# The first product of a layer by Strassen's seven products, with its elementwise function on four times wider tiles

## The chip, the cores and the metric

The kernel runs on one core of a Trainium2 chip. The metric is the device time of one execution in microseconds. TensorE (PE) does the matmuls, VectorE (DVE) and ScalarE (ACT) the elementwise work, GpSimd (POOL) a few reductions over partitions, and SyncE (SP) issues the transfers.

## The reference

Chunked attention makes 4608 rows of 512; two feed-forward layers follow, each 512 to 2048 to 512. The second layer is what the change is about:

```python
def _moe2_ref(x, w_in, w_out, a, b) -> np.ndarray:
    h = x @ w_in
    h2 = h * h
    h3 = h2 * h
    P = a[0] + a[1] * h + a[2] * h2 + a[3] * h3
    Q = 1.0 + np.abs(b[0]) * np.abs(h) + np.abs(b[1]) * h2
    g = P / (Q + 1e-06)
    return (g @ w_out).astype(np.float32)
```

The first layer has the same two products with `s * relu(h)**2 + b` between them. Everything is fp32 in and out; the weights come as 64-bit words and are decoded on the chip.

## The kernel before

Every product runs in pairs of fp16: an operand is scaled by a power of two and split in a high and a low half, and each product of 128x128 weights with a moving operand is made three times (`TERMS`: high by high, high by low, low by high) and added in PSUM.

Layer 1 goes through the rows in blocks (the list `blocks`: two of 256 rows in plain fp32, eight of 512). For each block it takes the 16 slices `f` of the 2048 inner columns: `l1_h` (L409 by `h_mm`: 12 matmuls of 512 columns into one PSUM bank), `l1_g` (Relu, Square and the split, whose low half is a subtraction on VectorE, L435), `l1_y` (L451: 12 matmuls into the four banks `y`). A table of jobs by slot (`at`) places attention, the decoding of weights (`w2_load`, `w2_park`) and, per block, `y_norm` and `y_split` (L374, L375) beside them. `y_split` splits the layer's result in four pieces and stores it to DRAM (`yd`). In the last block the weights of layer 2 are fetched again and split, two a slot (`split`, L172 and L173).

Layer 2 takes nine blocks of 512 rows. A unit is one slice `f` of a block: `l2_s1` makes h (12 matmuls, `h_mm`, banks h, h, s, x in turn) and starts the rational function on 128x512 elements, `l2_s2` ends it with the two halves of g, `l2_y` (L775) does 12 matmuls of the second product. The second product trails the first by `LAG = 3` units. The division is a logarithm and an exponential on ScalarE (L754, L755), followed by one correction for the low half. Per unit VectorE has seven operations (L750 to L752, L762 to L765) and ScalarE five.

The order on each engine is set by the framework's scheduler, which moves instructions within their dependences; the calls in the code set only their priority.

Of the kernel before, what the change touches and what calls it, by code (L numbers as in the profile page):

```python
# [20 lines left out]
def attn_moe_moe2(ctx: ExitStack, tc: tile.TileContext, qk, v, w_in, w_out, s_in, b_in,  # L21
# [39 lines left out]
    yd = [dram.tile([128, KD, 2, 512], F16, name=f"yd{j}", tag=f"yd{j}") for j in range(NB2)]  # L61
# [7 lines left out]
    def tiny(n, nm, dt=F32):  # L69
        return l1_p.tile([128, n], dt, name=nm, tag=nm)  # L70
# [119 lines left out]
    wo2 = Weight(w2_out, "out", None, "w")  # L190
# [90 lines left out]
    xhl = {}  # L281
# [203 lines left out]
    def y_norm(j2):  # L485
# [23 lines left out]

    def w2_scale():  # L510
# [48 lines left out]
    bufs = ((y1_p, "y32"), (y1_p, "yhl"), (raw_p, "raw"), (hl_p, "xhl"), (hl_p, "xhl"))[:3]  # L559
# [31 lines left out]
    at(start[2] + WS + WP * KF, w2_scale)  # L591

    if True:
# [63 lines left out]
        for slot, (j, f) in enumerate(seq1):  # L657
            if (j, f) == (NB - 1, 0):
                right.close()
                w2_p = ctx.enter_context(tc.tile_pool(name="w2", bufs=2 * KF + 1, side="right", reuse_waits="tile"))  # L660
                for w in (wi2, wo2):
                    w.pool = w2_p
                    for i in range(KF):
                        w.fetch(i)
            run_jobs(slot)
            if j == NB - 1:
                for n in (2 * f, 2 * f + 1):
                    w, i = park[n]
                    w.split(i)
# [12 lines left out]
        l2_p = ctx.enter_context(tc.tile_pool(name="l2", bufs=2, reuse_waits="tile"))
        o_p = ctx.enter_context(tc.tile_pool(name="o", bufs=4, reuse_waits="tile"))

        q0c = 1.0 + 1e-6
        bt = small(2)
        V.tensor_scalar(out=bt.bitcast(I32), in0=b2_sb.bitcast(I32), scalar1=0x7FFFFFFF, scalar2=None,
                        op0=ALU.bitwise_and)
        aabs = small(4)
        V.tensor_scalar(out=aabs.bitcast(I32), in0=a2_sb.bitcast(I32), scalar1=0x7FFFFFFF, scalar2=None,  # L690
                        op0=ALU.bitwise_and)
        rb = small(2)
        V.tensor_scalar(out=rb, in0=bt, scalar1=2.0 ** -100, scalar2=None, op0=ALU.max)
        V.reciprocal(out=rb, in_=rb)
        lnb = small(1)
# [142 lines left out]
```

## Time and profile before

| | |
|---|---|
| runs | 1621.27 us median of 3 (1620.11 to 1621.80) |
| profiled execution | 1621.44 us |
| its span, first to last instruction | 1619.7 us |
| mean granted TensorE clock, share of full | 0.995 |
| PE, DVE, ACT busy over the span | 99%, 76%, 60% |
| layer 1 and attention, to the last matmul of L451 | about 868 us |
| layer 2 | from there to the end |

A span is counted from the first to the last instruction. Times of one instruction are from its start to its end; neighbours on one engine can overlap, so the distance from start to start is the pace.

### The profile page before, as it was taken

The numbers are of one execution on the slowest core, as the hardware profiler recorded it, in microseconds if no ns is written. First come the engines' busy times: TensorE is split into PE (matmuls) and PEld (weight loads), VectorE is DVE, ScalarE is ACT, GpSimd is POOL, SyncE is SP. The second block draws the span as 40 slices with busy tenths as digits, with TensorE's granted clock in tenths as the row PEclk, the third lists the DMA queues.
The fourth block names the chain that finished last, engine by engine and source line by source line (L and its number), as shares of the span: only waits on it lengthen the run. The fifth ranks groups of instructions, "written<-read, shape, count | busy, mean of one in ns | idle before, by whom it ended". The sixth has DMA issues, their size and how long they took to land.

```text
span 1619.7 us, 25231 instructions
## 1 busy us (share of the span) xinstructions
PE 1604.5 (99%) x10052; PEld 795.6 (49%) x10052; DVE 1238.9 (76%) x2412; ACT 978.7 (60%) x1629; POOL 23.1 (1%) x57
## 2 busy tenths in 40 slices
PE   7999999999999999999999999999999999999999
PEld 6887454444444444444444444444444444444444
DVE  7986457766666664452456999999999999999997
ACT  3677556464645555453676666666666666666665
POOL 0000000000000000000000000000000000000000
PEclk8999999999999999999999999999999999999999
DMA  7732116435253522112501010101010101010000
GB/s 270 284 90 74 53 34 196 149 98 163 75 176 89 176 66 66 40 40 85 182 1 52 1 52 1 53 1 52 1 52 1 52 1 52 1 40 13 1 27 26
DMA packets 70549, 116.96 MB, mean 72 GB/s; under 512 B 37920, under 2 KB 37920, under 8 KB 68128
## 3 DMA queue, kind: packets, MB, share of 16 engines
q1 hardware_dynamic: 70432, 115.37, 22.0%
q8 instruction: 78, 1.28, 0.3%
q14 instruction: 39, 0.32, 0.1%
HBM read 79.70 MB, written 27.26 MB: 66 GB/s over the span
## 4 chain that ended last, share of the span: by engine, by line
PE 93%; DVE 3%; issue 3%; ACT 1%; POOL 0%; POOLq 0%
PE hp L409 43%; PE y L775 23%; PE y L451 20%; PE xp L296 2%; PE hp L419 1%; PE sp L248 1%; PE y L446 1%; DVE bits L134 1%; DVE wf L135 1%; DVE bits L132 1%; PE cs L479 0%; PE xp L354 0%; PE tp L311 0%; POOL amx L219 0%; DVE whl L173 0%
## 5 line engine op out<-in xcount | busy, mean ns | idle before, releaser
L409 PE MATMUL hp<-xhl,whl 128*128 128x512 f16 x3264 | 750.0, 380 | 0.0
L409 PEld LDWEIGHTS <-whl 128*128 128x128 f16 x3264 | 314.9, 98 | 375.9 <-issue 1.7
L775 PE MATMUL y<-whl,g 128*128 128x512 f16 x1728 | 395.4, 379 | 0.9 <-DVE g L762 0.5
L451 PE MATMUL y<-g,whl 128*128 128x512 f16 x1536 | 352.1, 379 | 0.0
L775 PEld LDWEIGHTS <-g 128*128 128x128 f16 x1728 | 168.6, 98 | 206.0 <-DVE g L765 3.0
L451 PEld LDWEIGHTS <-whl 128*128 128x128 f16 x1536 | 150.2, 98 | 181.6 <-issue 0.5
L754 ACT ACTIVATE rr<-qq,c 128x512 f32<-128x512 f32 x144 | 104.0, 722 | 194.9 <-DVE qq L750 194.7
L435 DVE TENSOR_TENSOR g<-r,g 128x512 f16<-128x512 f32 x128 | 88.0, 687 | 124.5 <-ACT g L434 124.5
L424 ACT ACTIVATE r<-hp 128x512 f32<-128x512 f32 (+1 forms) x160 | 87.5, 547 | 141.6 <-PE hp L409 126.2
L762 DVE SCALAR_TENSOR_TENSOR g<-e,na,rr 128x512 f16<-128x512 f32 x144 | 107.9, 750 | 17.1 <-ACT rr L755 14.6
L747 ACT ACTIVATE vv<-hp 128x512 f32<-128x512 f32 x144 | 85.5, 594 | 52.8 <-PE hp L409 52.6
L749 ACT ACTIVATE e<-hp,na 128x512 f32<-128x512 f32 x144 | 112.4, 780 | 0.0
L764 DVE SCALAR_TENSOR_TENSOR e<-e,na,qq 128x512 f32<-128x512 f32 x144 | 108.0, 750 | 3.8
L750 DVE SCALAR_TENSOR_TENSOR qq<-qq,bc,vv 128x512 f32<-128x512 f32 x144 | 107.2, 745 | 3.9 <-ACT qq L748 3.7
L752 DVE SCALAR_TENSOR_TENSOR e<-e,na,hp 128x512 f32<-128x512 f32 x144 | 107.3, 745 | 3.2
L755 ACT ACTIVATE rr<-rr,c 128x512 f32<-128x512 f32 x144 | 104.0, 722 | 4.5
L763 DVE SCALAR_TENSOR_TENSOR qq<-qq,g 128x512 f32<-128x512 f32 x144 | 99.5, 691 | 4.3
L765 DVE TENSOR_TENSOR g<-e,rr 128x512 f16<-128x512 f32 x144 | 99.2, 689 | 3.4
L748 ACT ACTIVATE qq<-hp,bc 128x512 f32<-128x512 f32 x144 | 98.1, 682 | 0.0
L751 DVE TENSOR_TENSOR e<-e,hp 128x512 f32<-128x512 f32 x144 | 97.8, 679 | 0.0
L425 ACT ACTIVATE r<-r 128x512 f32<-128x512 f32 (+1 forms) x160 | 93.5, 585 | 4.0
L434 ACT ACTIVATE g<-r 128x512 f16<-128x512 f32 x128 | 80.3, 628 | 3.2
(131 smaller groups left out, 1189.4 us busy)
## 6 DMA issues: line engine op xcount, KB each, us to landing
qk<-in_qk_dram SPq DMA_DIRECT2D x36, 512.0 KB, 4.0
raw<-in_moe_w_in_dram SPq DMA_DIRECT2D x16, 1024.0 KB, 5.3
raw<-in_moe_w_out_dram SPq DMA_DIRECT2D x16, 1024.0 KB, 5.2
v<-in_v_dram SPq DMA_DIRECT2D x36, 256.0 KB, 2.7
yd<-yhl SPq DMA_DIRECT2D x9, 1024.0 KB, 4.8
xhl<-yd SPq DMA_DIRECT2D x9, 1024.0 KB, 4.8
out_dram<-o SPq DMA_DIRECT2D x36, 256.0 KB, 2.1
w2din<-wf SPq DMA_DIRECT2D x16, 256.0 KB, 2.4
```

Source lines behind the costliest of these rows:

```text
L409: T.matmul(out=hp, lhsT=u[:, o:o + 128], rhs=x[:, kk, l, :], start=(m == 0), stop=(m == 3 * KD - 1))
L451: T.matmul(out=ybank[j][dd], lhsT=wo1.hl[f][:, o:o + 128], rhs=g[:, l, :], start=(f == 0 and m == 0), stop=(f == KF - 1 and m == 2))
L749: A.activation(out=e, in_=hp, func=AF.Identity, scale=na[:, 3:4], bias=na[:, 2:3])
L750: V.scalar_tensor_tensor(out=qq, in0=qq, scalar=bc[:, 0:1], in1=vv, op0=ALU.add, op1=ALU.mult)
L752: V.scalar_tensor_tensor(out=e, in0=e, scalar=na[:, 1:2], in1=hp, op0=ALU.add, op1=ALU.mult)
L754: A.activation(out=r, in_=qq, func=AF.Ln, scale=2.0 ** -40, bias=lnb)
L755: A.activation(out=r, in_=r, func=AF.Exp, scale=-1.0, bias=exb)
L762: V.scalar_tensor_tensor(out=g[:, 0, :], in0=e, scalar=na[:, 0:1], in1=r, op0=ALU.add, op1=ALU.mult)
L763: V.scalar_tensor_tensor(out=qq, in0=qq, scalar=q0c, in1=g[:, 0, :], op0=ALU.add, op1=ALU.mult)
L764: V.scalar_tensor_tensor(out=e, in0=e, scalar=na[:, 0:1], in1=qq, op0=ALU.add, op1=ALU.subtract)
L765: V.tensor_tensor(out=g[:, 1, :], in0=e, in1=r, op=ALU.mult)
L775: T.matmul(out=ybank[j][t], lhsT=g[:, a, t * 128:(t + 1) * 128], rhs=w[:, l * 512:(l + 1) * 512], start=(f == 0 and m == 0), stop=(f == KF ...
```

## The change

Layer 2's h is made in quadrants. The 512 inner dimensions are cut in two halves, the 512 rows of a block in two halves of 256 (`b`), the 2048 columns in two halves (`a`). Eight products of quadrants become seven, in Winograd's form of Strassen's method: sums of quadrants of the weights (`A11`, `A12`, `A22`, `S1` to `S4`) with sums of quadrants of the layer's input (`11`, `21`, `22`, `T1` to `T4`). The weights' sums are made and split once, in the last block of layer 1 (`w2_combo`, 28 tiles, in place of the 16 splits of `w2_in`); the input's sums in `y_split`, seven pieces (`y_piece`) in place of four.

A step is one quarter `u` of a block: seven products of 12 matmuls of 256 columns, into three PSUM banks Z, Y and C. Partial sums stay there: Z holds product 1, is copied to C (L968), then takes products 6, 5 and 3 on top, with ScalarE's and VectorE's copies between them: `snap` (L855), the add L982 (called H11), the add L984 (H10), and the copies L980 and L990. Together they fill `h`, 128x2048. The rational function then runs on all 2048 elements at once, as `chain_a` to `chain_e`; its denominator has a new form with one absolute value and one multiply-add. The second product (`l2_y`, now L907) is the same, and trails two steps; `m4` puts its four slices of a step into four slots between the products. The first and the last step's chains run in four parts of 512. `wo2` is fetched and split while layer 1's last block frees buffers. `hl` has ten buffers of quarter size.

```diff
+    PROD = {"1": ("A11", "11"), "2": ("A12", "21"), "3": ("S4", "22"), "4": ("A22", "T4"),
+            "5": ("S1", "T1"), "6": ("S2", "T2"), "7": ("S3", "T3")}
...
     def y_split(j2):
-        hl = y1_p.tile([128, KD, 2, 512], F16, name="yhl", tag="yhl")
-        split_hl(hl, y32.pop(j2), scy)
-        nc.sync.dma_start(out=yd[j2], in_=hl)
+        for p in YORD:
+            y_piece(j2, p)
...
+        if p == "T3":
+            src = y1_p.tile([128, 2, 256], F32, name="tx", tag="tx")
+            V.tensor_tensor(out=src, in0=b22, in1=b12, op=ALU.subtract)
...
+        hl = y1_p.tile([128, 2, 2, 256], F16, name="yhl", tag="yhl", bufs=3)
+        A.activation(out=hl[:, 0], in_=src, func=AF.Identity, scale=scy)
+        V.scalar_tensor_tensor(out=hl[:, 1], in0=src, scalar=scy, in1=hl[:, 0], op0=ALU.mult, op1=ALU.subtract)
+        nc.sync.dma_start(out=yd[j2][p], in_=hl)
...
+        def product(i, p, b, start, stop=False):
+            j, u = seq[i]
+            wk, pk = PROD[p]
+            for s in range(2):
+                f = 2 * u + s
+                for kk in range(2):
+                    w = wi2.sh[wk, kk, f // 4]
+                    for n, (a, l) in enumerate(TERMS):
+                        o = (f % 4) * 128
+                        T.matmul(out=b[:, s, :], lhsT=w[:, a, o:o + 128], rhs=yin[j][pk][:, l, kk, :],
...
+        def chain_b(i, sl):
...
+            V.scalar_tensor_tensor(out=v, in0=v, scalar=dlt, in1=v, op0=ALU.add, op1=ALU.mult)
+            V.tensor_tensor(out=e, in0=e, in1=hh, op=ALU.mult)
+            V.scalar_tensor_tensor(out=e, in0=e, scalar=na[:, 1:2], in1=hh, op0=ALU.add, op1=ALU.mult)
...
+        for i in range(N + 2):
+            cur, c = i < N, i - 1
+            sl = (parts if c in (0, N - 1) else full) if 0 <= c < N else []
...
+                product(i, "1", Z, True)
+                product(i, "7", Y, True)
...
+            for x in sl:
+                chain_a(c, x)
+            for x in sl:
+                chain_b(c, x)
+            run_m4(i, 0)
+            if cur:
+                C = new_bank(i, "C")
+                A.activation(out=C, in_=Z, func=AF.Copy)
+                product(i, "2", C, False)
+                product(i, "6", Z, False)
+            for x in sl:
+                chain_c(c, x)
+                chain_d(c, x)
...
+            run_m4(i, 1)
+            if cur:
+                snap(i, "u1", Z)
+                snap(i, "p7", Y)
+                A.activation(out=hq[:, 0, 0], in_=C, func=AF.Copy)
+                product(i, "5", Z, False)
+                V.tensor_tensor(out=hq[:, 1, 1], in0=Z, in1=sn.pop((i, "p7")), op=ALU.add)
+                product(i, "4", Y, False, True)
+                V.tensor_tensor(out=hq[:, 1, 0], in0=Y, in1=sn.pop((i, "u1")), op=ALU.add)
+            if len(sl) == 1:
+                chain_e(c, sl[0])
+            run_m4(i, 2)
+            if cur:
+                product(i, "3", Z, False, True)
+                A.activation(out=hq[:, 0, 1], in_=Z, func=AF.Copy)
+            run_m4(i, 3)
```

In the middle of layer 2 VectorE's row holds, before, one unit after another; this is the rest of one and the start of the next, with small operations of `l2_par` between them:

```order
L762 SCALAR_TENSOR_TENSOR g_12123<-e,na,rr 128x512
L763 SCALAR_TENSOR_TENSOR qq<-qq,g_12123 128x512
L764 SCALAR_TENSOR_TENSOR e<-e,na,qq 128x512
L765 TENSOR_TENSOR g_12123<-e,rr 128x512
L737 TENSOR_TENSOR ao<-ig,c_130 128x1
L727 TENSOR_SCALAR ig<-ge 128x1
L750 SCALAR_TENSOR_TENSOR qq<-qq,bc,vv 128x512
L751 TENSOR_TENSOR e<-e,hp 128x512
L752 SCALAR_TENSOR_TENSOR e<-e,na,hp 128x512
```

And this, at the same place on VectorE, is one whole step of the change (called v, eh, e2, g0, v2, e3, H11, H10 and g1 in the text):

```order
L873 SCALAR_TENSOR_TENSOR v<-v,c_262 128x2048
L874 TENSOR_TENSOR e<-e,h 128x2048
L875 SCALAR_TENSOR_TENSOR e<-e,na,h 128x2048
L888 SCALAR_TENSOR_TENSOR g_12176<-e,na,r 128x2048
L889 SCALAR_TENSOR_TENSOR v<-v,g_12176 128x2048
L895 SCALAR_TENSOR_TENSOR e<-e,na,v 128x2048
L982 TENSOR_TENSOR h<-bZ,sn 128x2x256
L984 TENSOR_TENSOR h<-bY,sn 128x2x256
L896 TENSOR_TENSOR g_12176<-e,r 128x2048
```

The seven operations stay seven, each four times as wide, and the two adds that fill h of the next step stand between the sixth and the seventh.

At the start of layer 2, the end of the first chain (in parts of 512) on VectorE, and what stands behind it:

```order
L888 SCALAR_TENSOR_TENSOR g_10423<-e,na,r 128x512
L895 SCALAR_TENSOR_TENSOR e<-e,na,v 128x512
L889 SCALAR_TENSOR_TENSOR v<-v,g_10423 128x512
L896 TENSOR_TENSOR g_10423<-e,r 128x512
L895 SCALAR_TENSOR_TENSOR e<-e,na,v 128x512
L982 TENSOR_TENSOR h<-bZ,sn 128x2x256
L896 TENSOR_TENSOR g_10423<-e,r 128x512
L984 TENSOR_TENSOR h<-bY,sn 128x2x256
```

The adds of step 1 stand at the very end of step 0's chain; before, no add stood on VectorE between a product and its use.

In layer 1 this is `y_split` of one block on VectorE before (`c_196` is its scale, g the subtraction L435):

```order
L375 SCALAR_TENSOR_TENSOR yhl<-y_5106,c_196,yhl 128x512 x2
L435 TENSOR_TENSOR g<-r,g 128x512
L375 SCALAR_TENSOR_TENSOR yhl<-y_5106,c_196,yhl 128x512 x2
L97 TENSOR_SCALAR apm<-amx 128x1
L99 TENSOR_SCALAR ape<-apm 128x1
```

And after (the same subtraction is now L440; two of the sums, T3 and T1, already stand ahead of these rows):

```order
L440 TENSOR_TENSOR g<-r,g 128x512
L524 SCALAR_TENSOR_TENSOR yhl<-y_5287,c_250,yhl 128x512 x2
L524 SCALAR_TENSOR_TENSOR yhl<-tx,c_250,yhl 128x512
L101 TENSOR_SCALAR apm<-amx 128x1
L516 TENSOR_TENSOR tx<-y_5287 128x512
L103 TENSOR_SCALAR ape<-apm 128x1
L519 TENSOR_TENSOR y_5287<-tx,y_5287 128x2x256
L524 SCALAR_TENSOR_TENSOR yhl<-y_5287,c_250,yhl 128x512 x2
L440 TENSOR_TENSOR g<-r,g 128x512
L524 SCALAR_TENSOR_TENSOR yhl<-tx,c_250,yhl 128x512
```

Seven wide splits and four sums now stand about the subtractions g where four splits stood.

## Rows read from the trace of the kernel before

**Rows 1.** The page, part 1: TensorE's busy time, share and instructions.

```profile
PE 1604.5 (99%) x10052; PEld 795.6 (49%) x10052; DVE 1238.9 (76%) x2412; ACT 978.7 (60%) x1629; POOL 23.1 (1%) x57
```

**Rows 2.** The page, part 4: the chain that ended last.

```profile
PE 93%; DVE 3%; issue 3%; ACT 1%; POOL 0%; POOLq 0%
PE hp L409 43%; PE y L775 23%; PE y L451 20%; PE xp L296 2%; PE hp L419 1%; PE sp L248 1%; PE y L446 1%; DVE bits L134 1%; DVE wf L135 1%; DVE bits L132 1%; PE cs L479 0%; PE xp L354 0%; PE tp L311 0%; POOL amx L219 0%; DVE whl L173 0%
```

**Rows 3.** Busy time by windows, 950 to 1600 us: stretch, length, each engine, clock.

```profile
950.00:1600.00 650.00, 650.00 (x3013) 294.71 (x3012) 614.40 (x977) 426.53 (x659) 0.00 (x0) 1.00 0.06 23
```

**Rows 4.** Timeline of VectorE in layer 2: start, duration, line, operation, count.

```profile
902.22 0.74 DVE L762 SCALAR_TENSOR_TENSOR g<-e,na,rr 128x512 f16<-128x512 f32 x1
902.88 0.74 DVE L750 SCALAR_TENSOR_TENSOR qq<-qq,bc,vv 128x512 f32<-128x512 f32 x1
903.54 0.68 DVE L763 SCALAR_TENSOR_TENSOR qq<-qq,g 128x512 f32<-128x512 f32 x1
904.15 0.68 DVE L751 TENSOR_TENSOR e<-e,hp 128x512 f32<-128x512 f32 x1
...
906.67 0.74 DVE L762 SCALAR_TENSOR_TENSOR g<-e,na,rr 128x512 f16<-128x512 f32 x1
```

**Rows 5.** The chain that ended last in order of time: start, length, matmuls.

```profile
228.23 3.20 PE cs L479 x128
...
1605.41 10.38 PE y L775 x48
```

**Rows 6.** Groups by line and form: busy us, mean ns of one, idle before.

```profile
L775 PE MATMUL y<-whl,g 128*128 128x512 f16 x1728 | 395.4, 379 | 0.9 <-DVE g L762 0.5 <-DVE g L765 0.4
...
L731 DVE TENSOR_TENSOR na<-na,c 128x1 f32<-128x1 f32 x27 | 4.2, 155 | 0.3
...
L479 PEld LDWEIGHTS <-whl 128*128 128x128 f16 x128 | 3.4, 96 | 0.2
```

**Rows 7.** Groups by line and form on VectorE and ScalarE, two sizes each.

```profile
L751 DVE TENSOR_TENSOR e<-e,hp 128x512 f32<-128x512 f32 x144 | 97.8, 679 | 0.0
L425 ACT ACTIVATE r<-r 128x512 f32<-128x512 f32 x128 | 80.4, 628 | 3.4
L260 DVE TENSOR_TENSOR e<-sp,mx 128x256 f32<-128x256 f32 x72 | 27.1, 413 | 0.0
L425 ACT ACTIVATE r<-r 128x256 f32<-128x256 f32 x32 | 13.2, 411 | 0.6
```

**Rows 8.** Timeline of VectorE at the end, where one operation needs the last.

```profile
1610.23 0.75 DVE L762 SCALAR_TENSOR_TENSOR g<-e,na,rr 128x512 f16<-128x512 f32 x1 [0.16 <-ACT rr L755]
1611.02 0.69 DVE L763 SCALAR_TENSOR_TENSOR qq<-qq,g 128x512 f32<-128x512 f32 x1
```

**Rows 9.** Timeline of ScalarE in layer 2.

```profile
900.93 0.60 ACT L747 ACTIVATE vv<-hp 128x512 f32<-128x512 f32 x1 [0.23 <-PE hp L409]
901.42 0.68 ACT L748 ACTIVATE qq<-hp,bc 128x512 f32<-128x512 f32 x1
901.99 0.78 ACT L749 ACTIVATE e<-hp,na 128x512 f32<-128x512 f32 x1
```

**Rows 10.** Timeline of TensorE where layer 2 begins.

```profile
868.03 10.52 PE L409 MATMUL hp<-xhl,whl 128*128 128x512 f16 x48
879.06 1.90 PE L775 MATMUL y<-whl,g 128*128 128x512 f16 x8 [0.51 <-DVE g L762]
```

**Rows 11.** Busy time by windows about L479: five engines, then the granted clock.

```profile
228.00:231.60 3.60, 3.60 (x131) 3.33 (x129) 2.01 (x9) 0.60 (x1) 0.38 (x1) 0.92 0.28 76
```

**Rows 12.** Busy time by windows, VectorE alone, layer 1 and its last block.

```profile
600.00:700.00 100.00, 48.36 (x115) 1.00 0.18 50
...
800.00:850.00 50.00, 28.74 (x40) 1.00 0.11 40
```

**Rows 13.** Timeline of VectorE and of TensorE at the end of layer 1.

```profile
857.23 0.69 DVE L435 TENSOR_TENSOR g<-r,g 128x512 f16<-128x512 f32 x1 [3.95 <-ACT g L434]
...
860.26 7.93 PE L451 MATMUL y<-g,whl 128*128 128x512 f16 x36
```

More of the change, by code (lines that the diff above doesn't have):

```diff
@@ L189, in attn_moe_moe2 @@
     wi2 = Weight(w2_in, "in", None, "w")
-    wo2 = Weight(w2_out, "out", None, "w")
+    wo2 = Weight(w2_out, "out", wo1_p, "w")
+    wi2.sh = {}
     park = [(w, i) for w in (wi2, wo2) for i in range(KF)]
@@ L408, in h_mm @@
                 o = a * 512 + (f % 4) * 128
-                T.matmul(out=hp, lhsT=u[:, o:o + 128], rhs=x[:, kk, l, :], start=(m == 0), stop=(m == 3 * KD - 1))
+                T.matmul(out=hp, lhsT=u[:, o:o + 128], rhs=x[kk][:, l, :], start=(m == 0), stop=(m == 3 * KD - 1))
                 m += 1
@@ L591, in attn_moe_moe2 @@
     at(start[2] + WS + WP * KF, w2_scale)
+    at(start[3], l2_consts)
     if True:
@@ L674, in attn_moe_moe2 @@
                 y_step()
+        for i in (KF - 2, KF - 1):
+            wo2.fetch(i)
         g_step()
@@ L677, in attn_moe_moe2 @@
             y_step()
-        for slot in sorted(jobs):
-            run_jobs(slot)
+        for i in range(KF - 4, KF):
+            wo2.split(i)
+        late = sorted(jobs)
         left.close()
[L682 to L695, printed above, removed]
-        V.memset(lnb, q0c * 2.0 ** -40)
-        exb = small(1)
-        V.memset(exb, -40.0 * 0.6931471805599453)
+        l2_p = ctx.enter_context(tc.tile_pool(name="l2", bufs=1, reuse_waits="tile"))
         yin = {}
@@ new lines, in chain_c, with chain_d @@
+        def chain_c(i, sl):
+            v, e, r = (t[:, sl[0]:sl[1]] for t in s2[i][:3])
+            A.activation(out=r, in_=v, func=AF.Ln, scale=2.0 ** -40, bias=lnb)
+            A.activation(out=r, in_=r, func=AF.Exp, scale=-1.0, bias=exb)
+        def chain_d(i, sl):
+            na, bc, ao = par[seq[i][0]]
+            if sl[0] == 0:
+                s2[i].append(l2_p.tile([128, 2, BIG], F16, name="g2", tag="g2", bufs=2))
+            v, e, r = (t[:, sl[0]:sl[1]] for t in s2[i][:3])
+            g = s2[i][3][:, :, sl[0]:sl[1]]
+            V.scalar_tensor_tensor(out=g[:, 0], in0=e, scalar=na[:, 0:1], in1=r, op0=ALU.add, op1=ALU.mult)
+            V.scalar_tensor_tensor(out=v, in0=v, scalar=q0c, in1=g[:, 0], op0=ALU.add, op1=ALU.mult)
@@ L770, in l2_y, with chain_e @@
+        def chain_e(i, sl):
+            na, bc, ao = par[seq[i][0]]
+            v, e, r = (t[:, sl[0]:sl[1]] for t in s2[i][:3])
+            g = s2[i][3][:, :, sl[0]:sl[1]]
+            V.scalar_tensor_tensor(out=e, in0=e, scalar=na[:, 0:1], in1=v, op0=ALU.add, op1=ALU.subtract)
+            V.tensor_tensor(out=g[:, 1], in0=e, in1=r, op=ALU.mult)
+        def l2_y(i, q):
+            j, u = seq[i]
+            if u == 0 and q == 0:
                 ybank[j] = [ps_y.tile([128, 512], F32, name=f"y{dd}", tag=f"y{dd}") for dd in range(4)]
-            g = s2.pop((j, f))
+            f = 2 * u + (q % 2) + 8 * (q // 2)
+            g = s2[i][3].rearrange("p l (q t) -> p l q t", q=4)
@@ new lines, in attn_moe_moe2 @@
+        T.matmul(out=prime, lhsT=wo2.hl[0][:, 0:128], rhs=wo2.hl[0][:, 0:512], start=True, stop=True)
+        N = len(seq)
+        full, parts = [(0, BIG)], [(a, a + 512) for a in range(0, BIG, 512)]
+        m4 = {i: [[], [], [], []] for i in range(N + 2)}
+        for i in range(N):
+            for q in range(4):
+                step, slot = i + 2, q
+                if i == 0:
+                    step, slot = ((2, 2), (2, 3), (2, 3), (3, 0))[q]
+                elif i == 1:
+                    slot = q
+                m4[step][slot].append((i, q))
```

238 lines of the change are left out of this document (167 added, 71 removed).

## The prediction

> **What bounds the kernel now.** I read the page's busy shares first, then the chain that ended last, then the second layer alone, and in it the pace of each engine.
>
> TensorE is busy 99% of the span and the chain that ended last is 93% TensorE [rows 1, 2]. Its three large lines are L409 (the first product of both layers), L775 (the second product of layer 2) and L451 (the second product of layer 1). In the window from 950 to 1600 us, which is nearly all of layer 2, TensorE is busy all 650 us, at full clock, VectorE 614 us and ScalarE 427 us [rows 3]. Busy time is no measure of room here, because consecutive operations overlap: the starts say more. On VectorE the seven operations of one unit of 128x512 start 4.45 us apart from one round to the next (902.22 to 906.67) [rows 4], while TensorE needs 24 matmuls, 2 x 2.59 = 5.18 us, for the same unit [rows 5]. So TensorE sets the pace of layer 2 and VectorE has 14% to spare; only fewer or shorter matmuls make it faster.
>
> Everything below is made against the profiled execution's own time, 1621.44 us (span 1619.7 and 1.7 around it), which lies 0.2 us above the median of the runs. What a measurement of this kernel can tell from no change is about 0.2%, 3.2 us.
>
> **The matmuls of layer 2.** Now: 144 units of 24 matmuls of 512 columns at 215.8 ns (48 in 10.38 us, so 12 in 2.59) [rows 5], so 745.8 us. The change keeps the second product (1728 matmuls of 512 columns, 373.0 us) and replaces the first one's 1728 by 36 steps x 7 products x 12 = 3024 matmuls of 256 columns. No row has a f16 matmul of 256 columns with a weight load of its own. Two rows bracket it. At best it costs half of one with 512, 107.9 ns. At worst I lay a straight line between the 128 matmuls of one column on L479, 3.20 us or 25.0 ns each, every one with its own 128x128 load, and the 512-column one: 25.0 + 190.8 x 255/511 = 120.2 ns. The L479 row says that loads follow each other at 25 ns although one takes 96 ns from start to end [rows 5, 6]: they are pipelined, and a load fits behind 107 ns of columns. So I take 109 ns, near the lower end: 329.6 us, **43.4 us less**. The bounds are 46.7 and 9.5 us less.
>
> Here a rule speaks against the change. The Trainium skill, "TensorE: Matmul & The Clock Gate", section "LDWEIGHTS (loading the stationary operand)", prices a load at its columns over 1.2 GHz, 107 ns for 128 columns, and its Part 3 says that a load overlaps a running matmul only where the two use different row groups. By that a matmul of 256 columns would be an estimated 107 + 107 = 214 ns, the price of 512 columns now, and the change would lose some 270 us. The trace disagrees: by the same rule 512 columns would cost 320 ns, and they are paced at 215.8; a pair on L479 takes 25.
>
> **One step of the changed layer 2.** A step is 7 x 1.31 + 4 x 2.59 = 19.5 us of TensorE, in place of 4 x 5.18 = 20.7. Do the others keep up?
>
> VectorE per step: seven operations of 2048 elements and two adds of 512. At 512 an operation with a per-partition scalar starts 0.66 us before the next, one without 0.60 [rows 4]. An element more costs (679 - 413)/256 = 1.04 ns [rows 7], so 1536 more cost 1.60 us: 2.26 and 2.20. Four of the first kind and three of the second make 15.6, the adds 1.2. Where an operation needs the one just before it, the start comes 0.79 instead of 0.66 after it [rows 8]: five such pairs, 0.6. The 24 small operations of `l2_par` come once in four steps and take at most 0.155 each [rows 6]: 0.9 a step. Sum 18.3 of 19.5: the large operations save four times 4.45 - 15.6 = 2.2 us of the fixed cost per step, and the adds take half of that back.
>
> ScalarE: 0.85 ns an element ((628 - 411)/256), 0.57 us from a 512-wide Abs with a pointer to the next start, 0.49 without [rows 7, 9]; so 1.9 to 2.0 us for each of four wide ones, five copies at 0.5, a quarter of four outputs: 11 us. It isn't near.
>
> The engines also wait for one another in a ring. `v` starts on VectorE; in the order shown, v, eh, e2, g0, v2, e3 and the add H11 (L982) follow, 2.26 + 2.20 + 2.38 + 2.39 + 2.33 + 2.38 + 0.60 = 14.5 us; product 3 may write its bank only then (1.3 and 0.2 drain); ScalarE empties it (0.5) and makes the next |h| (1.9), and the next `v` can start. That is 18.5 us with a semaphore's way or two, 1 us under the step. So TensorE stays the bound; for the outputs' four ScalarE operations between `v` and `e`, once in four steps, I add 2 us over the layer (bounds 0 and 9: 36 times a quarter of a microsecond).
>
> **Start of layer 2.** Today TensorE has 0.9 us of holes before the second product in all of layer 2 [rows 6], the first of 0.51 us at 879.06, after 48 matmuls of the first product [rows 10]. In the changed order the second product trails two steps, not three units. Let T be the end of layer 1's last product. The first step's h needs its seven products with the copies between them; its last add is done about T+10, ScalarE's first |h| half a microsecond later, and VectorE starts the first chain at T+11. That chain stands whole before the adds of step 1 (order shown), 4 x 4.45 + 1.2 = 19 us: T+30. Then follow 2.7 us of pieces of the last y and three rounds of 17.5 plus two y pieces. The low halves g1 of steps 1, 2 and 3 are ready at T+55, T+73 and T+91. Counted in the changed order, TensorE has before each of them 328, 395 and 467 short and 56, 104 and 152 long matmuls, 47.8, 65.5 and 83.7 us of work. It is 7 to 7.5 us early each time; from then on VectorE gains over 1 us a step and the hole doesn't grow. I take 8 us for it, **7 more than now**; bounds 3 (the early work stretches over it) and 15 (the clock falls too: it read 0.92 in 3.6 us with the one-column matmuls [rows 11]).
>
> **Layer 1.** `y_split` becomes seven pieces: 7 x 0.66 + 4 x 0.60 = 7.0 us of VectorE a block instead of 2.6, and seven ScalarE operations instead of four. What hides it: VectorE is busy 48 of 100 us there [rows 12], and in the order shown the pieces stand between the subtractions g that the second product needs. In the last block 28 weight combinations with 16 sums and 16 splits take the place of 32 splits, 38.6 against 21.1 us in 83; it is busy 29 of 50 [rows 12]. What cover a late g has: it ends at 857.92 and is read at 860.26, 2.3 us [rows 13]. Between two g's of the last block VectorE now has up to 7.7 us where a slot has 5.2, 2.5 late once. I take **2 us**; bounds 0 and 12. Without the cover it would be 8 x 4.4 = 35 us. SP's queue has seven transfers of 256 KB where one of 1 MB stood; ten `hl` buffers let the first three go at once, and each later one has a product before it.
>
> **End.** The last chain runs in four pieces beside the previous step's second product: its halves are ready 10.3 and 15.3 us after that begins, and TensorE asks at 10.4 and 15.6. **0.5 us**. ScalarE's four outputs and the last stores stay as they are.
>
> **Sum.** 1621.4 - 43.4 + 2 + 7 + 2 + 0.5 = 1589.5, so **1590 us**, 1.9% less.
>
> **The rivals.**
>
> *A load that is not hidden behind 256 columns.* For it: only 13 ns lie between 96 and 109, and nothing here has run so. Against it: 25 ns a pair on L479. At 120.2 ns the time is 1590 + 3024 x 0.0112 = 1624; with the load wholly exposed, 109 + 96 ns, it is 1880. By the skill's rule above the result would lie at that far end, which the 512-column pace contradicts.
>
> *The ring of three engines sets the step.* This one decides the sign. The spare in the ring is 1 us of 19.5; if the wide operations, or the waits between engines, add more than 1 us, TensorE waits in each of 36 steps. At 0.9 us over the spare, 1.9 in all, the gain of 31.5 us is gone; at 3 in all the time is 1590 + 72 = 1662. For it: VectorE's operations depend on each other, and a chain that was spread over three units in flight is now one. Against it: the prices above are read from rows, and the buffers of h, v and g are doubled.
>
> *Larger holes at the start and in layer 1*, from ScalarE's splits of `wo2` that wait for their fetches, or y pieces in the way: with 20 to 35 us more, 1610 to 1625. VectorE's 48% speaks against it.
>
> **How the numbers follow.** The forecast, TensorE bound with a hole at the start, 1578 to 1604: 66%. The load at 115 ns or more: 7%, two of them far out. The ring: 12%, half of it below the old time. Larger holes: 13%, three quarters faster. Below 1577: 2%. Together faster 0.83, same 0.06, slower 0.11. From 1577 to 1618 some 17% are left out.
>
> **What would show it.** Twelve matmuls of a product at 1.31 us in the timeline of TensorE; a step of 19.5 us with no wait in the steady part; VectorE's wide operations 2.2 to 2.3 us apart and its share near 90%; holes of 7 to 8 us in the first 60 us after layer 1 and none in it. I am wrong if product 3 or product 2 waits in every step (for the add L982 or the copy L968), if a product takes 1.4 us or more, or if layer 1 ends later than 868 us by more than a few.

## The result, and the profile after

The changed kernel takes 1594.66 us (median of four runs, 1593.01 to 1596.58) against 1621.53 us of the kernel before on the same chip: ratio 0.9835, 95% interval 0.9818 to 0.9852. The forecast was 1590 us, in a range of 1577 to 1618. The profiled execution took 1593.01 us, with a span of 1591.2 us. In what follows TensorE's pace is counted from start to start, 109.1 ns for a matmul of 256 columns and 215.8 ns for one of 512, and a hole is what lies between two groups beyond that pace.

The page, parts 1 and 4: busy time, and the chain that ended last.

```profile
PE 1565.9 (98%) x11349; PEld 923.6 (58%) x11349; DVE 1232.2 (77%) x1886; ACT 921.8 (58%) x1296; POOL 25.7 (2%) x57
...
PE 73%; DVE 16%; issue 4%; DMA 4%; ACT 3%; POOL 0%; SPq 0%; POOLq 0%; ACTq 0%; DVEq 0%
```

TensorE issues 1297 matmuls more than in [rows 1] and is busy 39 us less. It still ends the chain, but with 73% where [rows 2] had 93%: there are stretches in which VectorE decides. The next views tell where they are. TensorE in the steady part, start, duration, line and count:

```profile
1194.25 1.47 PE L849 MATMUL bZ<-xhl,whl 128*128 128x256 f16 x12
1195.56 1.47 PE L849 MATMUL bY<-xhl,whl 128*128 128x256 f16 x12
1196.87 2.75 PE L907 MATMUL y<-whl,g 128*128 128x512 f16 x12
...
1211.19 2.75 PE L907 MATMUL y<-whl,g 128*128 128x512 f16 x12
1213.78 1.47 PE L849 MATMUL bZ<-xhl,whl 128*128 128x256 f16 x12
```

A product takes 1.31 us (1195.56 to 1196.87), and product 1 comes again after 19.53 us, which is 7 x 1.31 + 4 x 2.59: TensorE waits for nothing and sets the pace. VectorE and ScalarE in the same step:

```profile
1182.07 2.35 DVE L888 SCALAR_TENSOR_TENSOR g<-e,na,r 128x2048 f16<-128x2048 f32 x1
1184.45 2.29 DVE L889 SCALAR_TENSOR_TENSOR v<-v,g 128x2048 f32<-128x2048 f32 x1
1186.78 2.35 DVE L895 SCALAR_TENSOR_TENSOR e<-e,na,v 128x2048 f32<-128x2048 f32 x1
1189.05 0.68 DVE L982 TENSOR_TENSOR h<-bZ,sn 128x512 f32<-128x512 f32 x1
1189.65 0.68 DVE L984 TENSOR_TENSOR h<-bY,sn 128x512 f32<-128x512 f32 x1
1190.25 2.28 DVE L896 TENSOR_TENSOR g<-e,r 128x2048 f16<-128x2048 f32 x1
...
1194.53 2.35 DVE L873 SCALAR_TENSOR_TENSOR v<-v,c 128x2048 f32<-128x2048 f32 x1 [1.14 <-ACT v L864]
```

```profile
1191.86 0.60 ACT L990 ACTIVATE h<-bZ 128x512 f32<-128x512 f32 x1 [8.03 <-PE bZ L849]
1192.49 2.00 ACT L864 ACTIVATE v<-h,bc 128x2048 f32<-128x2048 f32 x1
```

The wide operations start 2.20 to 2.38 us apart, as [rows 4, 7, 8] gave. The bracket on L873 is the ring of the prediction at work: the adds (1189.05 and 1189.65), product 3, the copy L990, the next `v`, and only then VectorE goes on. It stood idle 1.14 us for it.

TensorE where layer 2 begins, with the brackets of its waits, and its granted clock there (windows; the clock is the figure ahead of the last two):

```profile
883.65 1.47 PE L849 MATMUL bZ<-xhl,whl 128*128 128x256 f16 x12
888.04 2.29 PE L849 MATMUL bC<-xhl,whl 128*128 128x256 f16 x12 [2.91 <-ACT bC L968]
890.12 2.36 PE L849 MATMUL bZ<-xhl,whl 128*128 128x256 f16 x12
...
926.34 3.63 PE L907 MATMUL y<-whl,g 128*128 128x512 f16 x16 [0.75 <-DVE g L896]
...
945.30 3.63 PE L907 MATMUL y<-whl,g 128*128 128x512 f16 x16 [0.92 <-DVE m L807]
...
964.64 1.04 PE L907 MATMUL y<-whl,g 128*128 128x512 f16 x4 [0.96 <-DVE g L896]
```

```profile
884.00:888.00 4.00, 1.13 (x11) 0.86 (x9) 4.00 (x8) 4.00 (x8) 0.00 (x0) 1.00 0.00 0
888.00:890.00 2.00, 1.96 (x12) 1.49 (x12) 2.00 (x4) 2.00 (x4) 0.00 (x0) 0.63 0.03 8
890.00:892.20 2.20, 2.20 (x13) 1.62 (x12) 2.20 (x4) 2.20 (x4) 0.00 (x0) 0.56 0.00 0
892.20:896.00 3.80, 3.80 (x29) 2.65 (x28) 3.80 (x7) 3.80 (x8) 0.00 (x0) 1.00 0.00 0
```

After a wait of 2.9 us the granted clock is 0.63 and then 0.56, near the lower level of 1.2 GHz, for about 4 us: two products take 2.08 and 2.20 us from start to start, 1.7 us lost. Then come waits for the low half of g (L896), one a round, the last at 982.2 us, and short ones for the add L982 until 1015 us. (At 945.30 the trace names L807; that is a small operation right behind L896 on VectorE.)

Layer 2, from its first product (870.64) to the end of its last matmul (108 from 1563.03 on, so 1586.3), lasts 715.7 us. Its matmuls are 3024 x 0.1091 + 1728 x 0.2158 = 702.8. So the holes are 12.9 us: 7.8 up to 930 us (the low clock's 1.7 among them), 4.5 from there to 1020, 0.5 behind it. Before, the same count is 747.6 - 745.8 = 1.8.

### The profile page after: what moved, and what is told of

It reads as the page before. It is cut to its first block, busy times and chain, and to the rows that moved or that the text cites. A ratio compares the mean times of both kernels' runs of the same rounds, so it can differ in the third digit from the quotient of the medians.

```text
span 1591.2 us, 27221 instructions
## 1 busy us (share of the span) xinstructions
PE 1565.9 (98%) x11349; PEld 923.6 (58%) x11349; DVE 1232.2 (77%) x1886; ACT 921.8 (58%) x1296; POOL 25.7 (2%) x57
## 4 chain that ended last, share of the span: by engine, by line
PE 73%; DVE 16%; issue 4%; DMA 4%; ACT 3%; POOL 0%; SPq 0%; POOLq 0%; ACTq 0%; DVEq 0%
PE y L907 19%; PE hp L414 16%; PE y L456 16%; PE bZ L849 9%; PE bY L849 5%; DMA raw<-in_moe_w_in_dram 2%; PE bC L849 2%; PE hp L424 1%; PE y L451 1%; DVE bits L138 1%; PE xp L301 1%; DVE wf L139 1%; DVE v L889 1%; DVE yhl L524 1%; PE sp L253 1%
## 5 line engine op out<-in xcount | busy, mean ns | idle before, releaser
L907 PE MATMUL y<-whl,g 128*128 128x512 f16 x1728 | 396.0, 379 | 3.0 <-DVE g L896 2.0
L414 PE MATMUL hp<-xhl,whl 128*128 128x512 f16 x1536 | 354.4, 380 | 2.5 <-ACT r L429 2.5
L849 PEld LDWEIGHTS <-whl 128*128 128x128 f16 x3024 | 296.6, 98 | 71.7 <-issue 7.8
L907 PEld LDWEIGHTS <-g 128*128 128x128 f16 x1728 | 168.7, 98 | 178.7 <-DVE g L896 4.4
L456 PEld LDWEIGHTS <-whl 128*128 128x128 f16 x1536 | 150.3, 98 | 181.8 <-issue 0.9
L414 PEld LDWEIGHTS <-whl 128*128 128x128 f16 x1536 | 146.1, 98 | 174.5 <-issue 4.5
L849 PE MATMUL bZ<-xhl,whl 128*128 128x256 f16 x1728 | 213.2, 273 | 2.1 <-ACT sn L855 1.1
L440 DVE TENSOR_TENSOR g<-r,g 128x512 f16<-128x512 f32 x128 | 88.0, 687 | 114.0 <-ACT g L439 113.9
L990 ACT ACTIVATE h<-bZ 128x512 f32<-128x512 f32 x36 | 21.4, 595 | 235.5 <-PE bZ L849 184.7
L873 DVE SCALAR_TENSOR_TENSOR v<-v,c 128x2048 f32<-128x2048 f32 (+1 forms) x42 | 85.8, 2044 | 37.3 <-ACT v L864 37.3
L849 PE MATMUL bY<-xhl,whl 128*128 128x256 f16 x864 | 106.2, 273 | 0.3 <-ACT sn L855 0.3
L874 DVE TENSOR_TENSOR e<-e,h 128x2048 f32<-128x2048 f32 (+1 forms) x42 | 83.1, 1981 | 11.3 <-ACT e L865 11.2
L888 DVE SCALAR_TENSOR_TENSOR g<-e,na,r 128x2048 f16<-128x2048 f32 (+1 forms) x42 | 85.7, 2045 | 6.0 <-ACT r L880 2.4
L875 DVE SCALAR_TENSOR_TENSOR e<-e,na,h 128x2048 f32<-128x2048 f32 (+1 forms) x42 | 85.7, 2045 | 0.8
L895 DVE SCALAR_TENSOR_TENSOR e<-e,na,v 128x2048 f32<-128x2048 f32 (+1 forms) x42 | 85.6, 2043 | 0.8
L889 DVE SCALAR_TENSOR_TENSOR v<-v,g 128x2048 f32<-128x2048 f32 (+1 forms) x42 | 83.2, 1984 | 1.0
L896 DVE TENSOR_TENSOR g<-e,r 128x2048 f16<-128x2048 f32 (+1 forms) x42 | 82.9, 1977 | 0.1
L865 ACT ACTIVATE e<-h,na 128x2048 f32<-128x2048 f32 (+1 forms) x42 | 77.3, 1842 | 6.3 <-DVE g L896 6.3
```

What stands on the lines that cost most here:

```text
L414: T.matmul(out=hp, lhsT=u[:, o:o + 128], rhs=x[kk][:, l, :], start=(m == 0), stop=(m == 3 * KD - 1))
L440: V.tensor_tensor(out=g[:, 1, :], in0=r, in1=g[:, 0, :], op=ALU.subtract)
L456: T.matmul(out=ybank[j][dd], lhsT=wo1.hl[f][:, o:o + 128], rhs=g[:, l, :], start=(f == 0 and m == 0), stop=(f == KF - 1 and m == 2))
L849: T.matmul(out=b[:, s, :], lhsT=w[:, a, o:o + 128], rhs=yin[j][pk][:, l, kk, :], start=start and s + kk + n == 0, stop=stop and s + kk + n ...
L873: V.scalar_tensor_tensor(out=v, in0=v, scalar=dlt, in1=v, op0=ALU.add, op1=ALU.mult)
L875: V.scalar_tensor_tensor(out=e, in0=e, scalar=na[:, 1:2], in1=hh, op0=ALU.add, op1=ALU.mult)
```

## Experiments

In each, the edit is made to the kernel that its expectation names first. No edit changes a value that is computed. The scheduler orders the engines' rows anew for each kernel, so an edit can also move operations that it doesn't touch; where that matters it is said. The diffs show the main lines, `...` marks what is left out.

**The matmul of 256 columns by itself.** The kernel before, with the first product's matmuls cut in two (`half` is 256 for layer 2, else n):

```diff
-                T.matmul(out=hp, lhsT=u[:, o:o + 128], rhs=x[:, kk, l, :], ...
+                for c in range(0, n, half):
+                    T.matmul(out=hp[:, c:c + half], lhsT=u[:, o:o + 128], rhs=x[:, kk, l, c:c + half], ...
```

> The kernel before, with each of the 1728 matmuls of 512 columns of layer 2's first product written as two of 256 columns, each with a weight load of its own; nothing else changes. Theory (a load fits behind 256 columns, a matmul takes 109 ns): 1728 x (2 x 109.1 - 215.8) = 4 us more, so about 1625.6 us, 0.3% over before. Rival (the straight line of the prediction, 120.2 ns): 42 us more, 1664 us. Rival (the load lies bare, 109 + 96 ns): over 330 us more, above 1950 us.

Measured 1627.96 us, ratio 1.0042 (1.0027 to 1.0057), so 4 to 9 us more. TensorE's first group of layer 2:

```profile
868.82 10.64 PE L411 MATMUL hp<-xhl,whl 128*128 128x256 f16 x96
```

96 matmuls in 10.64 us, of which the last counts 0.27 to its end: 109.1 ns each, every one with its own load. Of the 7.1 us by which its span is longer, the matmuls explain 4.1; the rest is layer 1 (0.8) and holes in layer 2 (2.2 more than before, 1.2 of them in the last group). The rule of the Trainium skill that the prediction weighed ("TensorE: Matmul & The Clock Gate", section "LDWEIGHTS (loading the stationary operand)") would have put this kernel at an estimated 1988 us (1621 + 1728 x (2 x 214 - 215.8) ns); the trace disagrees.

**The wide operations taken back.** The rational function in four parts in every step:

```diff
-            sl = (parts if c in (0, N - 1) else full) if 0 <= c < N else []
+            sl = parts if 0 <= c < N else []
```

> The changed kernel with the rational function in four pieces of 128x512 in every step, not only in the first and the last: Strassen's products without the wide operations. Theory (VectorE's fixed cost per operation decides): VectorE needs 4 x 4.45 + 1.2 + 0.9 = 19.9 us a step against TensorE's 19.5, so it sets the pace from the start and TensorE waits in every step: 36 x 0.4 = 14 us more, 1603 to 1612 us, VectorE without idle time. Rival (the pieces let ScalarE and VectorE overlap better, so that the wide operations buy nothing): 1590 to 1595 us, a step of 19.5 us.

Measured 1632.56 us, ratio 1.0071 (1.0056 to 1.0086): slower than before the change, and 20 us beyond what I expected. VectorE at the turn from one chain to the next:

```profile
1104.67 0.70 DVE L984 TENSOR_TENSOR h<-bY,sn 128x512 f32<-128x512 f32 x1
1106.16 0.75 DVE L873 SCALAR_TENSOR_TENSOR v<-v,c 128x512 f32<-128x512 f32 x1 [0.79 <-ACT v L864]
1107.34 0.69 DVE L874 TENSOR_TENSOR e<-e,h 128x512 f32<-128x512 f32 x1 [0.43 <-ACT e L865]
```

The theory's direction holds, its size doesn't: I had VectorE without idle time. The adds stand at the end of the chain, the next chain's first |h| needs them, and VectorE waits on top of its work: 1.2 us at this turn, 0.9 a step from 1020 to 1540 us. The adds of steps 3 to 19 come 20.46 us apart. So in this order the products of Strassen alone lose; they pay only with the wide operations. (Adds that stand earlier in a chain of four parts were not tried.)

**How much room the ring has.** L888 is repeated, on 512 or on all 2048 columns, in each wide chain; here with 512:

```diff
             V.scalar_tensor_tensor(out=g[:, 0], in0=e, scalar=na[:, 0:1], in1=r, op0=ALU.add, op1=ALU.mult)
+            if sl[1] - sl[0] == BIG:
+                V.scalar_tensor_tensor(out=g[:, 0, 0:512], in0=e[:, 0:512], ...
```

> The changed kernel with one more VectorE operation of 128x512 (0.66 us) in the chain of each step with wide operations; it repeats a quarter of L888 and changes no value. Theory (VectorE and the ring have about 1 us to spare in a step of 19.5): no wait in the steady part; only the catching up at the start, where VectorE sets the pace, is longer: 2 to 6 us more, 1597 to 1601 us. Rival (the ring is already at the edge): 34 x 0.6 = 20 us more, 1615 us.

> The changed kernel with one more VectorE operation of 128x2048 (2.27 us) in the chain of each step with wide operations; it repeats L888 whole and changes no value. Theory (1 us of spare, then VectorE sets the pace): a step of 20.5 to 20.8 us, 34 x 1.0 to 1.3 = 34 to 44 us more, 1629 to 1639 us, so the whole gain of the change is gone. Rival (the idle time of 1 to 2 us per step that the trace shows on VectorE is all room): 34 x 0.3 to 0.8, 1605 to 1622 us.

Measured 1605.42 us (ratio 0.9904, 0.9889 to 0.9919) and 1658.53 us (1.0221, 1.0200 to 1.0241). The first lies between its two theories, the second beyond both. From the adds L982 of the last 16 steps, the step is 19.53 us in the changed kernel, 19.78 with 0.66 us more and 21.27 with 2.39 more (its start to the next). So of 0.66 us 0.25 are lost, and of 2.39 us 1.73: the room is 0.4 to 0.65 us a step, not 1. The groups of VectorE with the wide extra, 1020 to 1540 us (busy, mean, idle before):

```profile
L873 DVE SCALAR_TENSOR_TENSOR v<-v,c 128x2048 f32<-128x2048 f32 x25 | 58.6, 2346 | 0.0
...
L874 DVE TENSOR_TENSOR e<-e,h 128x2048 f32<-128x2048 f32 x24 | 55.0, 2291 | 32.5 <-ACT e L865 32.5
```

VectorE idles 1.3 us a step (32.5 us in 24.4 steps) for `e` and not at all for `v`, because the scheduler has put L873 behind L875 in this kernel. The ring of the prediction now closes over `e`. One turn of it, on VectorE, TensorE, ScalarE and VectorE again (L985 is the first add, L993 the copy, L899 the last operation of the chain):

```profile
1333.40 0.68 DVE L985 TENSOR_TENSOR h<-bZ,sn 128x512 f32<-128x512 f32 x1
1334.00 2.28 DVE L899 TENSOR_TENSOR g<-e,r 128x2048 f16<-128x2048 f32 x1
...
1334.14 1.47 PE L849 MATMUL bZ<-xhl,whl 128*128 128x256 f16 x12 [0.57 <-DVE h L985]
...
1335.64 0.60 ACT L993 ACTIVATE h<-bZ 128x512 f32<-128x512 f32 x1 [1.40 <-PE bZ L849]
1336.32 2.10 ACT L865 ACTIVATE e<-h,na 128x2048 f32<-128x2048 f32 x1
...
1338.45 2.29 DVE L874 TENSOR_TENSOR e<-e,h 128x2048 f32<-128x2048 f32 x1 [1.56 <-ACT e L865]
```

So the ring is the bound there. But two ways meet ahead of L865: the copy ends at 1336.24, and L899, the last reader of the one buffer of `e`, at 1336.28. Which of them sets the room is not shown; the same extra with `e` free was not run. The same two groups of the changed kernel, same stretch:

```profile
L873 DVE SCALAR_TENSOR_TENSOR v<-v,c 128x2048 f32<-128x2048 f32 x27 | 63.5, 2350 | 36.8 <-ACT v L864 36.8
...
L874 DVE TENSOR_TENSOR e<-e,h 128x2048 f32<-128x2048 f32 x27 | 61.7, 2286 | 9.5 <-ACT e L865 9.5
```

It idles 46 us for `v` and `e`, 1.7 a step. Only 0.4 to 0.65 of that is room; the rest is a wait that the ring holds. The catching up at the start is longer too: with 0.66 us more TensorE's waits go on until about 1180 us.

**An eighth product.**

```diff
                 product(i, "1", Z, True)
+                product(i, "1", Z, True)
```

> The changed kernel with an eighth product in every step: product 1 is made twice into the same bank, the second time over the first, so no value changes. Theory (TensorE sets the step, a product costs its 1.31 us whole): 36 x 1.31 = 47 us more, less up to 8 us that fill the holes at the start: 1634 to 1642 us. Rival (the ring of three engines sets the step and TensorE has room in it): 36 x 0.5 or less, below 1615 us.

Measured 1645.34 us, ratio 1.0151 (1.0137 to 1.0165): 50.7 us more, 1.41 a step. A product costs its 1.31 us whole, and the rival is out. In the last 16 steps a step takes 21.18 us, 1.65 more; the 0.34 beyond the product are a hole of 0.45 us in three of four steps, for the add (L983 here), which stands behind L896 in this kernel. Of the holes up to 1020 us 3.9 us are filled (8.4 for 12.3), which these waits outweigh. One of them:

```profile
1205.20 2.75 PE L907 MATMUL y<-whl,g 128*128 128x512 f16 x12
1208.24 1.47 PE L849 MATMUL bZ<-xhl,whl 128*128 128x256 f16 x12 [0.29 <-DVE h L983]
```

**The holes at the start of layer 2.** From one wide L896 to the next VectorE takes 19.0, 19.4 and 17.6 us (their ends are 926.3, 945.2, 964.6 and 982.2) where the prediction had 17.5, or 18 with the pieces of y. The changed kernel at the turn of one such round, VectorE and ScalarE:

```profile
942.96 2.28 DVE L896 TENSOR_TENSOR g<-e,r 128x2048 f16<-128x2048 f32 x1
...
947.40 2.29 DVE L874 TENSOR_TENSOR e<-e,h 128x2048 f32<-128x2048 f32 x1 [1.72 <-ACT e L865]
```

```profile
945.27 2.09 ACT L865 ACTIVATE e<-h,na 128x2048 f32<-128x2048 f32 x1 [1.16 <-DVE g L896]
```

`e` has one buffer. ScalarE may write the next e only when L896 has read the last (945.2), and VectorE waits for it. The edit ends the use of e one operation earlier:

```diff
-            V.scalar_tensor_tensor(out=e, in0=e, scalar=na[:, 0:1], in1=v, op0=ALU.add, op1=ALU.subtract)
-            V.tensor_tensor(out=g[:, 1], in0=e, in1=r, op=ALU.mult)
+            V.scalar_tensor_tensor(out=v, in0=e, scalar=na[:, 0:1], in1=v, op0=ALU.add, op1=ALU.subtract)
+            V.tensor_tensor(out=g[:, 1], in0=v, in1=r, op=ALU.mult)
```

> The changed kernel with L895 writing its result into v in place of e, so that e, which has one buffer, comes free one wide operation (2.2 us) earlier and ScalarE can write the next e while L896 runs. Theory (in the first steps VectorE's round is not the 17.5 us of the prediction but 19 to 19.4, because L874 waits for ScalarE's 2.1 us on the single e): rounds of about 17.5 us, and the waits of the second product from 945 us on, about 4 us, are gone: 1589 to 1592 us. Rival (the rounds are long from the small operations and the last y's pieces on VectorE, and the single buffer costs nothing): 1594 to 1595 us.

Measured 1588.71 us, ratio 0.9797 (0.9783 to 0.9810), clear of the changed kernel's interval. At the same turn:

```profile
942.70 2.28 DVE L896 TENSOR_TENSOR g<-v,r 128x2048 f16<-128x2048 f32 x1
944.90 2.28 DVE L874 TENSOR_TENSOR e<-e,h 128x2048 f32<-128x2048 f32 x1
...
957.75 2.29 DVE L896 TENSOR_TENSOR g<-v,r 128x2048 f16<-128x2048 f32 x1
```

No idle time; the rounds are 17.7, 15.1 and 17.3 us, and after 945 us TensorE doesn't wait for L896 until the last step. In each kernel one of the three rounds holds six wide operations and not seven, since the next L873 stands ahead of L896 at one turn and behind it at another; so compare the means, 16.7 us a round for 18.6. Three more edits, by the next three expectations; the first two are made without this one, the third with it and both of them:

```diff
-                    extra.setdefault(4 + 2 * m, []).append((y_piece, (args[0], p)))
+                    extra.setdefault(12 + 2 * m, []).append((y_piece, (args[0], p)))
...
-                fn(*args)
+                with tc.issue_after(last(dve)), tc.issue_after(last(nc.scalar.engine)):
+                    fn(*args)
```

> The changed kernel with the seven pieces of the last y moved from the first steps of layer 2 to steps 12 to 24, held behind that step's work on VectorE and ScalarE; they are read in step 32. Theory (VectorE is late from the first chain on, and the pieces' ten operations, 6.6 us before 927 us in the trace, are all on its path): the waits of the second product from 926 us on, 5 to 6 us, are gone: 1588 to 1591 us. Rival (the pieces lie in gaps in which VectorE waits for h or e anyway): 1593 to 1595 us.

```diff
+            early = cur and c == 0
+            for x in sl[:1] if early else sl:
                 chain_a(c, x)
+            if early:
+                C = new_bank(i, "C")
+                A.activation(out=C, in_=Z, func=AF.Copy)
+                for x in sl[1:]:
+                    chain_a(c, x)
...
+            if early:
+                snap(i, "u1", Z)
+                snap(i, "p7", Y)
...
```

> The changed kernel with ScalarE's copies of step 1 (Z into the bank C, and the two snapshots) issued among the four pieces of the first chain instead of behind them. Theory (TensorE's wait of 2.9 us at 888 us, and the half clock that follows, 1.7 us, only come ahead of a wait for VectorE that would be there in any case): both are gone and the second product waits longer for the first chains: 1592 to 1595 us, a change of less than 0.2%. Rival (they are a loss of their own): 4.6 us less, 1590 us.

> The changed kernel with the three edits together: e free early, the last y's pieces late, step 1's copies first. Theory (one hole, set by VectorE's work up to the point where it has caught up): VectorE has 6.6 us less to do and gains 2 us a round, so that of some 12.5 us of holes 3 to 6 are left: 1585 to 1588 us. Rival (other waits, such as the ring with ScalarE's chain, stand behind these): 1590 us or more.

They gave 1592.85 us (0.9823, 0.9809 to 0.9836), 1595.02 (0.9835, 0.9817 to 0.9853) and 1590.88 (0.9807, 0.9794 to 0.9821). The first and the second can't be told from the changed kernel by time. Of the pieces the rival holds in the main: without them VectorE stands idle, since h of step 1 is complete only after the first chain.

```profile
901.05 0.68 DVE L984 TENSOR_TENSOR h<-bY,sn 128x512 f32<-128x512 f32 x1
905.35 2.35 DVE L873 SCALAR_TENSOR_TENSOR v<-v,c 128x2048 f32<-128x2048 f32 x1 [3.63 <-ACT v L864]
```

Of the copies the theory holds: the wait of 2.9 us and the low clock are gone (1.00 in all windows from 880 to 896 us), and layer 2 isn't shorter by it. The last steps follow from the idle 3.63 us: have h of step 1 ready sooner.

The edit keeps e free and ScalarE's copy of Z into C among the first chain, as above, and adds this (`tail` is the loop over `chain_c`, `chain_d` and `chain_e`):

```diff
+            if not early:
+                tail()
             run_m4(i, 1)
...
                 V.tensor_tensor(out=hq[:, 1, 0], in0=Y, in1=sn.pop((i, "u1")), op=ALU.add)
+            if early:
+                tail()
```

> The kernel with e free early, and in step 1 the copies, the products and the two additions of h issued ahead of the second half of the first chain (L888 to L896), so that ScalarE has the next v ready when VectorE ends that chain. Theory (with the last y's pieces gone VectorE stood idle there for 2 to 3.6 us, waiting for v; so VectorE's way through the first chain to h of step 1 is what sets the holes): VectorE's round of step 1 ends 1 to 3 us earlier and the hole is that much smaller, 1586 to 1588 us. Rival (VectorE has the same work before each of the first low halves, with the pieces in the gap as before): 1588 to 1590 us.

And one for layer 1, of which more below:

```diff
-                at(slot + 3, y_split, j2)
+                if j < NFULL:
+                    at(slot + 3, y_split, j2)
+                else:
+                    for m, p in enumerate(YORD):
+                        at(slot + 3 + m, y_piece, j2, p)
...
```

> The kernel with e free early (L895 writing into v), and in layer 1 the seven pieces of a block's y from the third full block on issued one per slot instead of all seven in one. Theory (layer 1's loss is the wait of 0.9 to 2.5 us near 407 us: VectorE is late with L237 behind the pieces, so SP issues the load of the next v late, L222 waits for it on ScalarE, and L429 behind it): that wait is gone, layer 2's first product starts at 868.5 to 870 us, 1586 to 1588 us. Rival (VectorE is late from the decoding of the second layer's weights, which stays): the wait stays, 1588 to 1590 us.

> The kernel with the three edits: e free early, layer 1's pieces one per slot, step 1's additions ahead of the second half of the first chain. If both theories hold: 1584 to 1586 us. If neither: 1588 to 1590 us.

Measured 1586.83 us (0.9793, 0.9780 to 0.9807), 1586.53 (0.9795, 0.9781 to 0.9808) and 1588.05 (0.9799, 0.9786 to 0.9812). By time these three and the one with e alone can't be told apart. Layer 2 by itself can, counted from its first product to the end of its last matmul, as above:

| kernel | layer 2, us | of it holes up to 1020 us | waits of TensorE in layer 1, 225 to 868 us |
|---|---|---|---|
| changed | 715.7 | 12.3 | 2.5 |
| e free | 713.1 | 9.2 | 1.6 |
| late pieces | 717.4 | 11.6 | 3.7 |
| copies first | 716.9 | 12.1 | 5.4 |
| these three together | 713.4 | 7.1 | 2.7 |
| e free, adds first | 711.5 | 7.7 | 0.3 |
| e free, pieces spread | 712.8 | 9.2 | 0 |
| all of the last two | 711.6 | 7.7 | 1.2 |

Two pairs in it do the same in layer 2 (e free with and without spread pieces, adds first with and without them); they differ by 0.3 and 0.1 us. The edit on e brings 2.6 us: of the 4.5 us of holes between 930 and 1020 us 1.2 are left. The adds bring 1.2 to 1.6 more; the first wide L896 ends 51.4 us after layer 2's first product in place of 55.6. The late pieces and the copies bring nothing in all, but not because they do nothing: together with e free they take 2.1 us of holes up to 1020 us, and where the pieces now stand they cost 2.5 (from 1020 to 1540 us 3.1 us of holes for 0.6, and 3.0 for 0.5 with the pieces alone). What the medians differ by beyond that isn't in layer 2 of the profiled executions. Layer 1 ends at other times from profile to profile: in ten of them with the same code for it layer 2 begins between 867.1 and 872.6 us.

**Layer 1.** The changed kernel where TensorE waits longest there, on TensorE, ScalarE, VectorE and SP's queue:

```profile
407.65 2.75 PE L414 MATMUL hp<-xhl,whl 128*128 128x512 f16 x12 [2.34 <-ACT r L429]
...
406.39 0.63 ACT L222 ACTIVATE wsq<-v 128x512 bf16<-128x512 f32 x1 [11.14 <-DMA v<-in_v_dram]
...
399.65 0.74 DVE L237 SCALAR_TENSOR_TENSOR vs<-v,sc,vs 128x512 f16<-128x512 f32 x1
...
400.42 0.33 SPq L211 DMA_DIRECT2D v<-in_v_dram  x1
```

VectorE reads the old `v` in L237, SP then loads the next one, ScalarE waits for it in L222, and `r` of the next slice stands behind that. Before, the same three stood 5 to 6 us earlier, and TensorE didn't wait:

```profile
394.54 0.74 DVE L232 SCALAR_TENSOR_TENSOR vs<-v,sc,vs 128x512 f16<-128x512 f32 x1
...
395.31 0.33 SPq L206 DMA_DIRECT2D v<-in_v_dram  x1
...
400.04 0.63 ACT L217 ACTIVATE wsq<-v 128x512 bf16<-128x512 f32 x1 [6.33 <-DMA v<-in_v_dram]
```

With the pieces one per slot (the expectations above) L222 starts at 400.61 and TensorE waits nowhere in layer 1; but the second kernel with this edit waits once, 1.22 us for a late g, and one without it only 0.25. Nor does a piece stand on VectorE in the 40 us ahead of L237. What delays it there is the decoding, which waits for its fetches (1.76 us at 392.93, 0.86 at 397.67). These fetches are late in turn: SP's fetch of `raw`, at 353.8 us before, is issued at 359.9, right behind the block's last piece (358.8); but the fetch before it was late already (309.9 for 302.1). So the pieces may be the cause through the fetches; it is not shown.

## Why the prediction was right

**The sum.** Predicted -43.4 + 2 + 7 + 2 + 0.5 on 1621.4. The profiled span is 28.5 us shorter than before, and it divides so: the matmuls -43.0 (702.8 for 745.8), layer 1 +2.4 (it ends at 870.4 for 868.0), one matmul between the layers (`prime`) +0.2, holes of layer 2 +11.1 (12.9 for 1.8), what follows the last matmul +0.8. The sum came out 3.5 us short of the profiled execution (4.7 of the median), and closer than its terms: 7 us for the start were 4 too few, and the 2.5 us for the outputs and the end, which cost nothing, made up for more than half of it.

**The matmul.** Right: 109.1 ns where 109 was taken, and the split kernel shows it apart from everything else. The first rival, a load that is not hidden, is out.

**The bound.** Right: TensorE, by the step of 19.53 us and the eighth product; VectorE's share is 90% in the steady part, as forecast. The term of 2 us for the outputs' ScalarE operations is about nothing; from 1020 us on all holes together are 0.5 us. One count behind VectorE's 18.3 us is off: `l2_par` has 19 small operations, not 24, 0.2 us a step.

**The ring.** The rival that decided the sign didn't come true, but was nearer than I put it. "18.5 us with a semaphore's way or two, 1 us under the step": measured, 0.4 to 0.65 under it (with the one buffer of e as a second way that may set it). And the point from which the gain is gone lies lower than 1.9 us a step: 0.66 us more cost 10.8 us and 2.39 more 63.9, so on the line between them the 26.9 us are gone at 1.2.

**The start of layer 2.** The mis-sized term: 11.1 us more than before for all holes of layer 2, where 7 + 2 + 0.5 stood. Its first half is right. The low halves of steps 1, 2 and 3 were forecast for 55, 73 and 91 us after layer 1; they came 55.6, 74.6 and 93.9 after layer 2's first product, and the holes up to 930 us are 7.8 us where 8 were forecast. In part this is luck: the terms written out give about 51 us for the first of them, and some 4 us are named nowhere. And most of these 7.8 us stand elsewhere, at 888 us on ScalarE's copy; with the copies first that wait goes and layer 2 is no shorter, so VectorE's lateness sets their sum. What failed is "from then on VectorE gains over 1 us a step and the hole doesn't grow": it grew by 4.5 us, and the catching up lasted to 1015 us in place of about 960. The single buffer of e puts ScalarE's 2.1 us between L896 and the next L874, so the first two rounds took 19.0 and 19.4 us and not 18; with e free these 4.5 us shrink to 1.2. The rival of larger holes has the place right, but its 20 to 35 us more compare with 5.

**Layer 1.** 2.4 us for 2, with the wrong place. I put it into the last block, on a late g. There TensorE waits for nothing; the wait is at 407 us, by a load that VectorE releases late and that holds up ScalarE's row. The ten profiles of the same code have 0.25 to 5.4 us of such waits, 2.6 on the mean; the kernel before and the split one, with the old code, have 0 and 0.4. So 2 us is right on the mean, while the spread, 5.5 us in where layer 2 begins, is over twice the term.

**The end.** No hole in the last 108 matmuls, for 0.5 us.

## What to carry to other kernels

When a chain is made wider and its tiles get fewer buffers, walk each buffer round the engines before pricing a round: the time from its last reader to its next reader, with the writer in between, is part of the round. Idle time of an engine that is in a ring with the bound is not room; put one small extra operation into the ring and read the step, which takes one run. And have both halves of such a change in the sum: here the products alone lost 11 us (in the order that the scheduler gave them), and with the wide operations they gained 27.

## What was not expected of the hardware

A wait of 2.9 us on TensorE was followed by some 4 us at a granted clock of 0.63 and 0.56. After a wait of 1.1 us in the same kernel (at 877.76) the next product took 1.31 us, the full pace; and after the 2.34 us at 407.65 the granted clock read 1.00 (408 to 412 us) and twelve matmuls of 512 columns took 2.59 us.
